# Loading the last rows of w2: 128 overlapping rows in 128 partitions instead of 96 rows in 96 partitions

## The chip, the cores and the metric

One core of one Trainium2 chip runs the whole kernel. The metric is the device time of one execution in microseconds (us). The core has five instruction streams: TensorE (PE in the profile, its weight loads PEld), VectorE (DVE), ScalarE (ACT), GpSimd (POOL) and SyncE (SP). Transfers are carried out by the core's 16 DMA engines; SyncE, ScalarE and GpSimd only put them into queues. Semaphores order everything: an instruction may wait until a semaphore has reached a value, and adds to one when it is done.

## The reference

The kernel computes one decode step of a gated mix of two branches for a single token x of 512 numbers: attention over a cache of 32 heads with 4096 keys and values each (branch a), and a small network with a squared ReLU (branch b). All inputs are bf16. Only branch b is touched here.

```python
g = _sigmoid((x * gate_w).sum(-1, keepdims=True))
a = _A_ref(x, A_k_cache, A_v_cache, A_wq, A_wo)   # q = x @ wq; softmax(q k^T) v per head; @ wo
# branch b: w1 is 512 x 1376, w2 is 1376 x 512
h = jnp.einsum("bsd,df->bsf", x, w1) + b1
r = jnp.where(h > zero, h, zero)
h = r * r
b = jnp.einsum("bsf,fd->bsd", h, w2) + b2
return g * a + (1 - g) * b
```

## The kernel before

The kernel reads the caches of keys and values once, 78.3 MB with all the weights, and works on what has arrived. The 32 heads are taken in 8 tiles of 4 heads. A tile of keys (k) or values (v) is 4 MB: 128 partitions with 32 KB each. Tiles live in a ring of five slots. SyncE issues the loads in a written order (`LOADS`): k0, k1, then k and v alternating, and before the last tile v7 the entry "m", which is branch b's weights. Before an issue it waits until the slot's old tile has been used (`free`).

For each key tile, VectorE computes scores of 80 of the 128 key blocks (L717: a multiply and a sum along the row in one instruction), and TensorE does the other 48: it transposes them (L508), ScalarE copies them out of PSUM (L414), and TensorE multiplies with the queries (L523). ScalarE takes the exponentials (L433), and TensorE multiplies them with the value tiles (L554, `pv`). The work on values stands far behind the work on keys in TensorE's order, which is written out by hand.

The last value tile v7 is loaded in four parts, of 40, 36, 32 and 20 blocks (`PARTS`), each with a semaphore of its own, so that TensorE can begin when the first has landed. In the order of SyncE's queue the end is: w1 (L335, 11,008 bytes for each of 128 partitions), the first 1280 rows of w2 (L336, 10,240 bytes for each partition, ten rows side by side), the 96 rows of w2 that are left (L337, 1,024 bytes for each of 96 partitions), the four parts of v7 (L330; 10,240, 9,216, 8,192 and 5,120 bytes for each partition), and the last 512 rows of wo (L339, two loads of 384 and 128 rows with 1,024 bytes each). The rest of wo came earlier, in pieces that SyncE (L326) and GpSimd (L377) issued.

At the end TensorE works in this order: its part of wo's product with the heads 0 to 27 (L584), h of branch b (L599, `mlp_h`, 11 columns of 4 matmuls), the softmax denominators (L563), branch b's product with w2 (L611, `mlp_out`, 11 groups of 4 matmuls), the first two parts of v7 (L554), the part of wo's product that VectorE had summed (L590), the last two parts of v7 (L554), the last four heads' product with wo (L620, `out_b`), and the transpose of the result (L675). VectorE has in this time a share of wo's product (L778, L782), the bias of h (L757), the squared ReLU (L762) and the factor 1 - g (L766), which makes `hs`, and at the very end the heads' normalisation (L747), the sum (L820) and a copy (L822), and SyncE stores the result (L342).

h is kept with 128 partitions and 11 columns: column n below 10 has the elements n, n + 10, and so on of the first 1280, and column 10 has the 96 that are left, in partitions 0 to 95. `b1c` is b1 in the same layout: TensorE turns the row b1 into columns in PSUM (L467), VectorE clears b1c at the start (L681) and copies it out in two pieces (L701, L702). `omg` is 1 - g, the same number in every partition (L695). Two places wait for both copies of b1c: `started` (L310, SyncE and GpSimd wait there before the pieces of wo) and TensorE, before it reuses that bank of PSUM (L475). The names FG = 10 and FR = 96 are the full groups and the rest.

Of the kernel before, what the change touches and what calls it, by code (L numbers as in the profile page):

```python
# [5 lines left out]
def bass_gated_mix__gqa_block_cached__dense_activation_squared_relu__decode_kernel(  # L6
# [15 lines left out]
    fp32 = mybir.dt.float32  # L22
    bf16 = mybir.dt.bfloat16
    ALU = mybir.AluOpType
# [5 lines left out]
    DM = 512  # L30
    F = 1376
    FG = 10
    FR = F - FG * 128
    SCALE = float(D) ** -0.5


# [59 lines left out]
    def turns():  # L96
        at, out = 0, []
        for _, e, k, _, _ in RUNS:
            d = (e - at) % 16
            out.append((False, d) if d != 1 else (True, e))  # L100
            at = (e + k) % 16
        return out
# [29 lines left out]
    with ctx:  # L132
        def sb(name, shape, dt):
            return ctx.enter_context(nc.sbuf_tensor(name, shape, dt))
# [4 lines left out]
        def sem(name):  # L139
            return ctx.enter_context(nc.semaphore(name))  # L140
# [3 lines left out]
        def held(kind, j=0):  # L144
            return ring[:, AT[kind, j] % SLOTS, :]
# [4 lines left out]
        W2, W3 = 4 * F, 4 * F + FG * DM  # L150
        w1_sb = held("m")[:, 0:W2].rearrange("p (t n) -> p t n", t=4)
        w2a = held("m")[:, W2:W3].rearrange("p (g n) -> p g n", g=FG)
        w2b = held("m")[0:FR, W3:W3 + DM]
        W4 = W3 + DM
        W5 = W4 + NZ * DM
        wob_sb = held("m")[:, W4:W5].rearrange("p (h n) -> p h n", h=NZ)
# [7 lines left out]
        def early(p, n):  # L164
            at[0] += n
            return start[0:p, at[0] - n:at[0]]

        xrow, grow, b1r, b2r = early(1, DM), early(1, DM), early(1, F), early(4, 128)
# [5 lines left out]
        xcol = sb("xcol", [128, 4], bf16)  # L174
        xcolf = sb("xcolf", [128, 4], fp32)
        b1c = sb("b1c", [128, FG + 1], fp32)
# [22 lines left out]
        omg = sb("omg", [128, 1], fp32)  # L199
        hr = sb("hr", [128, FG + 1], fp32)  # L200
        hp = sb("hp", [128, FG + 1], fp32)
        hs = sb("hs", [128, FG + 1], bf16)
        b2g = sb("b2g", [128, 4], fp32)
        fin = sb("fin", [128, 4], bf16)

# [16 lines left out]
        H = pX[:, 256:256 + FG + 1]  # L222
        MO = pX[:, 288:292]
        B1 = pM[:, 288:288 + FG + 1]
# [8 lines left out]
        s_dz = sem("s_dz")  # L233
        s_b = sem("s_b")
        s_l = [sem(f"s_l{i}") for i in range(SLOTS)]
        s_w = [sem(f"s_w{n}") for n in range(3)]
# [8 lines left out]
        s_b1c = sem("s_b1c")  # L245
# [13 lines left out]
        s_g = sem("s_g")  # L259
# [24 lines left out]
        s_hs = sem("s_hs")  # L284
# [14 lines left out]
        def free(eng, n):  # L299
            if n < SLOTS:  # L300
                return
            kind, j = LOADS[n - SLOTS]
            if kind == "k":
                eng.wait_ge(s_sd, U * (j + 1))
                eng.wait_ge(s_t, 2 * U * (j + 1))
            elif kind == "v":
                eng.wait_ge(s_pv, U * (j + 1))


        def started(eng):  # L310
            eng.wait_ge(s_qps, NT)
            eng.wait_ge(s_g, 4)
            eng.wait_ge(s_b1c, 2)


        @block.sync
        def _(eng):
            for n, (kind, j) in enumerate(LOADS):
                free(eng, n)
                if n == SLOTS - 1:  # L320
                    started(eng)
                    for p, st, k, q in STRIPS[len(RUNS):]:
                        a, b = W[p:p + st * (k - 1) + 1:st, :], woa_v[q:q + k, :]
                        if k == 1:
                            a, b = [v.rearrange("p (a n) -> p a n", a=2) for v in (a, b)]
                        eng.dma_start(a, b).then_inc(s_wr, 16)  # L326
                if kind == "v" and j in PARTS:
                    for w in range(len(PARTS[j]) - 1):
                        part = slice(PARTS[j][w] * 128, PARTS[j][w + 1] * 128)
                        eng.dma_start(held("v", j)[:, part], v_v[j][:, part]).then_inc(s_vl[j, w], 16)  # L330
                elif kind in "kv":
                    eng.dma_start(held(kind, j), (k_v if kind == "k" else v_v)[j])\
                       .then_inc(s_l[n % SLOTS], 16)
                elif kind == "m":
                    eng.dma_start(held("m")[:, 0:W2], w1_v).then_inc(s_w[0], 16)  # L335
                    eng.dma_start(held("m")[:, W2:W3], w2_v).then_inc(s_w[1], 16)  # L336
                    eng.dma_start(w2b, B_w2[FG * 128:F, :]).then_inc(s_w[2], 16)  # L337
            for c in range(len(TS) - 1):
                eng.dma_start(wob_sb[:, TS[c]:TS[c + 1], :], wob_v[:, TS[c]:TS[c + 1], :])\  # L339
                   .then_inc(s_wo[c], 16)  # L340
            eng.wait_ge(s_f4, 1)
            eng.dma_start(out[0, 0, :].rearrange("(j p) -> j p", p=128), fin4).then_inc(s_out, 16)  # L342
# [46 lines left out]
        def _(eng):  # L389
# [33 lines left out]
            def exps(j):  # L423
# [7 lines left out]
                for r in range(R):  # L431
                    rows = slice(P * r, P * r + P)
                    eng.activation(E[rows, j % NE, :, r], S[rows, j % NS, :], ACT.Exp,  # L433
                                   bias=nM[rows, j:j + 1], scale=SCALE,
                                   accum_out=RS[rows, R * j + r:R * j + r + 1]).then_inc(s_e, 1)
# [17 lines left out]
        def _(eng):  # L453
# [3 lines left out]
            for t in range(4):  # L457
                mm = eng.matmul(XC[:, t:t + 1], xrow[:, t:DM:4], ident[0:1, 0:1], start=True, stop=True)
# [4 lines left out]
            eng.wait_ge(s_b, 32)  # L463
            eng.transpose(B2, b2r, ident[0:4, 0:4]).then_inc(s_b2, 1)
            for n in range(FG + 1):
                M = 128 if n < FG else FR
                mm = eng.matmul(B1[0:M, n:n + 1], b1r[:, n:FG * 128:FG] if n < FG else b1r[:, FG * 128:F],  # L467
                                ident[0:1, 0:1], start=True, stop=True)
            mm.then_inc(s_b1, 1)
            eng.wait_ge(s_wq, 16)  # L470
# [1 line left out]
            eng.wait_ge(s_ez, 1)  # L472


            read = [(s_b1c, 2)]  # L475

            def pm(sem, count):
                for w in read:
# [114 lines left out]
            def mlp_h():  # L593
                eng.wait_ge(s_w[0], 16)
                for n in range(FG + 1):
                    M = 128 if n < FG else FR
                    for t in range(4):
                        lhs = w1_sb[:, t, n:FG * 128:FG] if n < FG else w1_sb[:, t, FG * 128:F]
                        mm = eng.matmul(H[0:M, n:n + 1], lhs, xcol[:, t:t + 1],  # L599
                                        start=(t == 0), stop=(t == 3))  # L600
                mm.then_inc(s_h, 1)

            def mlp_out():
                eng.wait_ge(s_w[1], 16)
                eng.wait_ge(s_w[2], 16)
                eng.wait_ge(s_hs, 1)
                for n in range(FG + 1):
                    M = 128 if n < FG else FR
                    w = w2a[:, n, :] if n < FG else w2b
                    for j in range(4):  # L610
                        mm = eng.matmul(MO[:, j:j + 1], w[:, j * 128:(j + 1) * 128], hs[0:M, n:n + 1],  # L611
                                        start=(n == 0 and j == 0), stop=(n == FG and j == 3),
                                        skip_group_check=True)
                mm.then_inc(s_mo, 1)
# [47 lines left out]
            spread_a()  # L662
            out_a()
            mlp_h()
            den(NG - 1)
            mlp_out()
            for u in range((NT - 1) * U, NU):
                if u == NU - 2:
# [9 lines left out]
        @block.vector  # L678
        def _(eng):
            eng.memset(zeros, 0.0).then_inc(s_dz, 1)  # L680
            eng.memset(b1c[:, :], 0.0).then_inc(s_dz, 1)  # L681
            eng.wait_ge(s_dz, 2)
            eng.wait_ge(s_x, 32)
            eng.tensor_tensor_reduce(grow, xrow, grow, 1.0, 0.0, ALU.mult,
                                     ALU.add, zp[:, :]).then_inc(s_zp, 1)
# [12 lines left out]
            eng.tensor_scalar(b2g[:, :], B2, omg[:, 0:1], None, ALU.mult).then_inc(s_g, 1)  # L698

            eng.wait_ge(s_b1, 1)  # L700
            eng.tensor_copy(b1c[:, 0:FG], B1[:, 0:FG]).then_inc(s_b1c, 1)  # L701
            eng.tensor_copy(b1c[0:FR, FG:FG + 1], B1[0:FR, FG:FG + 1]).then_inc(s_b1c, 1)  # L702

            def qcol_copy(c):
                eng.wait_ge(s_q, c + 1)
# [20 lines left out]
            def gmax(j):  # L726
                eng.wait_ge(s_mt, j + 1)
                if j >= 2:
# [5 lines left out]
                eng.tensor_scalar(gx[0:1, j % 2, :].rearrange("a (r p) -> a r p", r=R),  # L734
                                  g.unsqueeze(2).to_broadcast([1, R, P]), -SCALE, None, ALU.mult)\
                   .then_inc(s_dg, 1)
# [15 lines left out]

            def mlp_bias():
                eng.wait_ge(s_h, 1)
                eng.wait_ge(s_b1c, 2)
                for p, n in cells:
                    eng.tensor_tensor(hr[p, n], H[p, n], b1c[p, n], ALU.add).then_inc(s_hv, 1)  # L757

            def mlp():
                eng.wait_ge(s_hv, 1)  # L760
                for p, n in cells:
                    eng.scalar_tensor_tensor(out=hp[p, n], in0=hr[p, n], scalar=0.0, in1=hr[p, n],  # L762
                                             op0=ALU.max, op1=ALU.mult).then_inc(s_hv, 1)
                eng.wait_ge(s_hv, 2)
                for p, n in cells:
                    eng.tensor_scalar(hs[p, n], hp[p, n], omg[p, 0:1], None, ALU.mult).then_inc(s_hs, 1)  # L766

            def rows_v():
                eng.wait_ge(s_ac, 3)
# [84 lines left out]
```

## Time and profile before

| What | Value |
|---|---|
| median of three runs | 193.84 us (193.66 to 194.28) |
| the profiled execution, its own time | 194.1 us |
| its span in the profile | 192.7 us |
| VectorE busy | 157.3 us (82%) |
| TensorE busy, weight loads | 111.8 us, 99.3 us |
| ScalarE busy, GpSimd busy | 84.4 us, 22.6 us |
| read from HBM | 78.32 MB, 406 GB/s over the span |
| TensorE's granted clock, mean | 0.584 of full speed |

The span is what the profiler records, from the first instruction to the last; the execution's own time has 1.4 us around it. The profile cuts the span in 40 equal slices of 4.8 us and gives for each the busy share of every engine, the share of the DMA engines and what they moved. The chain of waits is followed back from the last instruction: at each step to what released it, or to the instruction before it. In lines of the chain, "DMA ring<-in_A_v_cache_dram" is the time from a load's issue to its landing, "SPq" is SyncE issuing, and "issue" is time in which an engine waited for nothing that the profile shows. A group such as "L554 x17" is 17 instructions of line 554.

### The profile page before, as it was taken

Reading aid. Unit: us, or ns where it says so; the run is one execution under the profiler, and the core shown is the slowest. Engines: PE = TensorE matmul, PEld = TensorE weight load, DVE = VectorE, ACT = ScalarE, POOL = GpSimd, SP = SyncE. Lnnn points to the kernel's source line nnn. Section 1 sums busy time; section 2 is a strip of 40 time slices with the busy share of each in tenths; the row PEclk is TensorE's granted clock in tenths of the full one; section 3 lists DMA queues with packets and bytes.
Section 4 is the critical chain, followed back from the end, with each engine's and each line's share of the span. In section 5 each row is a group of like instructions: output and inputs, shape, how many; then the busy total and the mean of one; then the engine's idle time right before and its main releaser. Section 6 shows DMA issues by size and latency. Waiting matters only on the chain.

```text
span 192.7 us, 6055 instructions
## 1 busy us (share of the span) xinstructions
PE 111.8 (58%) x2082; PEld 99.3 (52%) x2082; DVE 157.3 (82%) x1357; ACT 84.4 (44%) x204; POOL 22.6 (12%) x56
## 2 busy tenths in 40 slices
PE   0129665545604644396569055925886489769755
PEld 0123343435503543296559045924876378658754
DVE  0220399999999999899999998998999799938821
ACT  2004776734833753087349132933644295031000
POOL 7760001994000000000000000000000000000000
PEclk9999998555555555555555555555555555555555
DMA  6999999999999999999999999999999999999990
GB/s 218 436 435 435 435 437 425 437 468 400 429 427 415 408 451 425 432 410 432 429 424 408 425 434 422 430 434 435 432 420 408 422 410 413 429 415 377 418 367 31
DMA packets 5456, 78.71 MB, mean 408 GB/s; under 512 B 1285, under 2 KB 1895, under 8 KB 2024
## 3 DMA queue, kind: packets, MB, share of 16 engines
q1 hardware_dynamic: 4452, 75.37, 92.6%
q0 software_dynamic: 960, 2.95, 3.9%
q8 instruction: 16, 0.26, 0.6%
q14 instruction: 14, 0.11, 0.1%
q10 hardware_dynamic: 14, 0.01, 0.0%
HBM read 78.32 MB, written 0.00 MB: 406 GB/s over the span
## 4 chain that ended last, share of the span: by engine, by line
DVE 48%; DMA 42%; PE 5%; SPq 2%; issue 2%; DVEq 0%
DVE ring L717 44%; DMA ring<-in_A_k_cache_dram 26%; DMA ring<-in_A_v_cache_dram 16%; PE pO L554 2%; DVE S L717 2%; PE pQ L590 1%; SPq L330 1%; PE KP L508 1%; SPq L336 1%; DVE gm L731 1%; DVE gx L734 0%; PE pQ L620 0%; PE pM L535 0%; PE pM L563 0%; SPq L337 0%
## 5 line engine op out<-in xcount | busy, mean ns | idle before, releaser
L717 DVE CUSTOM_DVE_ANT_0 ring<-ring,qb 128x128 bf16<-128x128 bf16 x640 | 137.2, 280 | 2.6 <-DMA ring<-in_A_k_cache_dram 2.6
L414 ACT ACTIVATE kT<-KP 128x768 bf16<-128x768 bf16 x64 | 48.1, 810 | 49.2 <-PE KP L508 48.8
L508 PE MATMUL KP<-ident,ring 128*128 128x128 bf16 x384 | 45.1, 302 | 23.2 <-DMA ring<-in_A_k_cache_dram 20.5
L508 PEld LDWEIGHTS KP<-ident,ring 128*128 128x128 bf16 x384 | 37.6, 140 | 25.4 <-DMA ring<-in_A_k_cache_dram 20.9
L717 DVE DVE_READ_ACCUMULATOR2_ANT S<- 128x1 f32 x640 | 48.8, 76 | 0.1
L554 PE MATMUL pO<-E,ring 128*128 128x4 bf16 x640 | 19.7, 166 | 4.0 <-DMA ring<-in_A_v_cache_dram 3.0
L554 PEld LDWEIGHTS pO<-E,ring 128*128 128x128 bf16 x640 | 18.9, 105 | 4.5 <-DMA ring<-in_A_v_cache_dram 3.2
L433 ACT ACTIVATE E<-S,nM 32x128 bf16<-32x128 f32 x32 | 18.5, 578 | 0.9
L554 PE MATMUL pX<-E,ring 128*128 128x4 bf16 x384 | 12.0, 167 | 1.6 <-DMA ring<-in_A_v_cache_dram 1.5
L554 PEld LDWEIGHTS pX<-E,ring 128*128 128x128 bf16 x384 | 11.6, 105 | 2.0 <-DMA ring<-in_A_v_cache_dram 1.8
L530 PE MATMUL pM<-identf,mp 128*1 128x128 f32 x8 | 3.1, 384 | 12.8 <-DVE mp L724 12.8
L535 PE MATMUL pM<-onesf,gx 1*128 1x1 f32 x16 | 4.7, 358 | 9.5 <-DVE gx L734 9.5
L535 PEld LDWEIGHTS pM<-onesf,gx 1*128 1x128 f32 x16 | 4.0, 307 | 10.5 <-DVE gx L734 10.5
L523 PE MATMUL pQ<-qcol,kT 128*128 128x4 bf16 x192 | 8.3, 169 | 1.1 <-ACT kT L414 1.1
L523 PEld LDWEIGHTS pQ<-qcol,kT 128*128 128x128 bf16 x192 | 8.0, 110 | 1.4 <-ACT kT L414 1.3
L782 DVE SCALAR_TENSOR_TENSOR ring<-W,o2f,ring 128x512 f32<-128x512 bf16 x11 | 8.3, 751 | 0.4
L425 ACT ACTIVATE nM<-pM 128x1 f32<-128x1 f32 x8 | 1.4, 171 | 15.6 <-PE pM L535 15.6
L433 ACT ACTIVATION_READ_ACCUMULATOR E<-S,nM 32x1 f32 x32 | 8.1, 252 | 0.0
L377 POOL DMA_DIRECT2D W<-in_A_wo_dram x14 | 8.0, 574 | 0.0
L530 PEld LDWEIGHTS pM<-identf,mp 128*1 128x1 f32 x8 | 0.7, 92 | 13.9 <-DVE mp L724 13.9
L523 PE MATMUL pS<-qcol,kT 128*128 128x4 bf16 x192 | 7.9, 168 | 0.0
L385 POOL MEMSET tick<- 1x1 f32 x1 | 0.1, 89 | 66.6 <-DMA W<-in_A_wo_dram 66.6
(83 smaller groups left out, 97.6 us busy)
## 6 DMA issues: line engine op xcount, KB each, us to landing
ring<-in_A_k_cache_dram SPq DMA_DIRECT2D x8, 4096.0 KB, 30.5
ring<-in_A_v_cache_dram SPq DMA_DIRECT2D x5, 4096.0 KB, 29.8
ring<-in_A_v_cache_dram SPq DMA_DIRECT2D x5, 1024.0 KB, 28.5
W<-in_A_wq_dram SPq DMA_DIRECT2D x1, 4096.0 KB, 12.5
ring<-in_A_v_cache_dram SPq DMA_DIRECT2D x2, 2048.0 KB, 27.8
W<-in_A_wo_dram POOLq DMA_DIRECT2D x2, 768.0 KB, 18.1
ring<-in_B_w_dram SPq DMA_DIRECT2D x1, 1376.0 KB, 24.8
ring<-in_B_w_dram SPq DMA_DIRECT2D x1, 1280.0 KB, 27.9
```

Source lines behind the costliest of these rows:

```text
L330: eng.dma_start(held("v", j)[:, part], v_v[j][:, part]).then_inc(s_vl[j, w], 16)
L336: eng.dma_start(held("m")[:, W2:W3], w2_v).then_inc(s_w[1], 16)
L377: eng.dma_start(W[p:p + st * (k - 1) + 1:st, :], woa_v[q:q + k, :], max_dma_last_dim=16384).then_inc(s_wp[n], 16)
L414: eng.activation(kT[:, n % NC, :], KP[n % 3][:, :], ACT.Copy).then_inc(s_ev, 1)
L433: eng.activation(E[rows, j % NE, :, r], S[rows, j % NS, :], ACT.Exp, bias=nM[rows, j:j + 1], scale=SCALE, accum_out=RS[rows, R * j + r:R * ...
L508: mm = eng.transpose(KP[n % 3][:, y * 128:(y + 1) * 128], held("k", j)[:, b * 128:(b + 1) * 128], ident[:, :])
L523: mm = eng.matmul(S2[j % 2][:, c:c + R], kT[:, n % NC, y * 128:(y + 1) * 128], qcol[:, R * j:R * j + R], start=True, stop=True)
L530: eng.transpose(MT[0:1, :], mp[:, j:j + 1], identf[:, :]).then_inc(s_mt, 1)
L535: eng.matmul(MB[:, j:j + 1], gx[0:1, j % 2, :], onesf[0:1, 0:1], start=True, stop=True).then_inc(s_mb, 1)
L554: mm = eng.matmul(O(R * j, R * j + R), held("v", j)[:, b * 128:(b + 1) * 128], E[:, j % NE, b, :], start=(b == 0), stop=(b == B - 1), skip ...
L717: ins = eng.tensor_tensor_reduce(kb, kb, qb[:, j, :], 1.0, 0.0, ALU.mult, ALU.add, S[:, j % NS, b:b + 1])
L782: eng.scalar_tensor_tensor(out=vsum[:, :], in0=wo_sb[:, TP + t, :], scalar=o2f[:, t:t + 1], in1=vsum[:, :], op0=ALU.mult, op1=ALU.add).the ...
```

## The change

The last load of w2 takes the last 128 rows, 1248 to 1375, into 128 partitions. The first 32 of them, rows 1248 to 1279, are also among the 1280 rows loaded by L336. Column 10 of h is computed for the same 128 elements, so that every matmul of branch b has 128 columns or 128 rows. A new tile `omw` is 1 - g in all 128 x 11 places but the first 32 partitions of column 10, where it is zero; `hs` is the product with omw in place of the product with omg, so the overlapping rows count once. b1c is filled completely by one copy, and need not be cleared; the two waits on it ask for one copy. VectorE gets one instruction more in all; the instructions of the other engines stay as many.

```diff
--- before.py
+++ after.py
@@ -31,6 +31,8 @@
     F = 1376
     FG = 10
     FR = F - FG * 128
+
+    FO = 128 - FR
     SCALE = float(D) ** -0.5
 
 
@@ -150,7 +152,7 @@
         W2, W3 = 4 * F, 4 * F + FG * DM
         w1_sb = held("m")[:, 0:W2].rearrange("p (t n) -> p t n", t=4)
         w2a = held("m")[:, W2:W3].rearrange("p (g n) -> p g n", g=FG)
-        w2b = held("m")[0:FR, W3:W3 + DM]
+        w2b = held("m")[:, W3:W3 + DM]
         W4 = W3 + DM
         W5 = W4 + NZ * DM
         wob_sb = held("m")[:, W4:W5].rearrange("p (h n) -> p h n", h=NZ)
@@ -200,6 +202,7 @@
         hr = sb("hr", [128, FG + 1], fp32)
         hp = sb("hp", [128, FG + 1], fp32)
         hs = sb("hs", [128, FG + 1], bf16)
+        omw = sb("omw", [128, FG + 1], fp32)
         b2g = sb("b2g", [128, 4], fp32)
         fin = sb("fin", [128, 4], bf16)
 
@@ -310,7 +313,7 @@
         def started(eng):
             eng.wait_ge(s_qps, NT)
             eng.wait_ge(s_g, 4)
-            eng.wait_ge(s_b1c, 2)
+            eng.wait_ge(s_b1c, 1)
 
 
         @block.sync
@@ -334,7 +337,7 @@
                 elif kind == "m":
                     eng.dma_start(held("m")[:, 0:W2], w1_v).then_inc(s_w[0], 16)
                     eng.dma_start(held("m")[:, W2:W3], w2_v).then_inc(s_w[1], 16)
-                    eng.dma_start(w2b, B_w2[FG * 128:F, :]).then_inc(s_w[2], 16)
+                    eng.dma_start(w2b, B_w2[F - 128:F, :]).then_inc(s_w[2], 16)
             for c in range(len(TS) - 1):
                 eng.dma_start(wob_sb[:, TS[c]:TS[c + 1], :], wob_v[:, TS[c]:TS[c + 1], :])\
                    .then_inc(s_wo[c], 16)
@@ -463,8 +466,7 @@
             eng.wait_ge(s_b, 32)
             eng.transpose(B2, b2r, ident[0:4, 0:4]).then_inc(s_b2, 1)
             for n in range(FG + 1):
-                M = 128 if n < FG else FR
-                mm = eng.matmul(B1[0:M, n:n + 1], b1r[:, n:FG * 128:FG] if n < FG else b1r[:, FG * 128:F],
+                mm = eng.matmul(B1[:, n:n + 1], b1r[:, n:FG * 128:FG] if n < FG else b1r[:, F - 128:F],
                                 ident[0:1, 0:1], start=True, stop=True)
             mm.then_inc(s_b1, 1)
             eng.wait_ge(s_wq, 16)
@@ -472,7 +474,7 @@
             eng.wait_ge(s_ez, 1)
 
 
-            read = [(s_b1c, 2)]
+            read = [(s_b1c, 1)]
 
             def pm(sem, count):
                 for w in read:
@@ -593,10 +595,9 @@
             def mlp_h():
                 eng.wait_ge(s_w[0], 16)
                 for n in range(FG + 1):
-                    M = 128 if n < FG else FR
                     for t in range(4):
-                        lhs = w1_sb[:, t, n:FG * 128:FG] if n < FG else w1_sb[:, t, FG * 128:F]
-                        mm = eng.matmul(H[0:M, n:n + 1], lhs, xcol[:, t:t + 1],
+                        lhs = w1_sb[:, t, n:FG * 128:FG] if n < FG else w1_sb[:, t, F - 128:F]
+                        mm = eng.matmul(H[:, n:n + 1], lhs, xcol[:, t:t + 1],
                                         start=(t == 0), stop=(t == 3))
                 mm.then_inc(s_h, 1)
 
@@ -605,10 +606,9 @@
                 eng.wait_ge(s_w[2], 16)
                 eng.wait_ge(s_hs, 1)
                 for n in range(FG + 1):
-                    M = 128 if n < FG else FR
                     w = w2a[:, n, :] if n < FG else w2b
                     for j in range(4):
-                        mm = eng.matmul(MO[:, j:j + 1], w[:, j * 128:(j + 1) * 128], hs[0:M, n:n + 1],
+                        mm = eng.matmul(MO[:, j:j + 1], w[:, j * 128:(j + 1) * 128], hs[:, n:n + 1],
                                         start=(n == 0 and j == 0), stop=(n == FG and j == 3),
                                         skip_group_check=True)
                 mm.then_inc(s_mo, 1)
@@ -678,8 +678,9 @@
         @block.vector
         def _(eng):
             eng.memset(zeros, 0.0).then_inc(s_dz, 1)
-            eng.memset(b1c[:, :], 0.0).then_inc(s_dz, 1)
+            eng.memset(omw[:, :], 1.0).then_inc(s_dz, 1)
             eng.wait_ge(s_dz, 2)
+            eng.memset(omw[0:FO, FG:FG + 1], 0.0).then_inc(s_dz, 1)
             eng.wait_ge(s_x, 32)
             eng.tensor_tensor_reduce(grow, xrow, grow, 1.0, 0.0, ALU.mult,
                                      ALU.add, zp[:, :]).then_inc(s_zp, 1)
@@ -698,8 +699,9 @@
             eng.tensor_scalar(b2g[:, :], B2, omg[:, 0:1], None, ALU.mult).then_inc(s_g, 1)
 
             eng.wait_ge(s_b1, 1)
-            eng.tensor_copy(b1c[:, 0:FG], B1[:, 0:FG]).then_inc(s_b1c, 1)
-            eng.tensor_copy(b1c[0:FR, FG:FG + 1], B1[0:FR, FG:FG + 1]).then_inc(s_b1c, 1)
+            eng.tensor_copy(b1c[:, :], B1).then_inc(s_b1c, 1)
+            eng.wait_ge(s_dz, 3)
+            eng.tensor_scalar(omw[:, :], omw[:, :], omg[:, 0:1], None, ALU.mult).then_inc(s_g, 1)
 
             def qcol_copy(c):
                 eng.wait_ge(s_q, c + 1)
@@ -752,7 +754,7 @@
 
             def mlp_bias():
                 eng.wait_ge(s_h, 1)
-                eng.wait_ge(s_b1c, 2)
+                eng.wait_ge(s_b1c, 1)
                 for p, n in cells:
                     eng.tensor_tensor(hr[p, n], H[p, n], b1c[p, n], ALU.add).then_inc(s_hv, 1)
 
@@ -762,8 +764,9 @@
                     eng.scalar_tensor_tensor(out=hp[p, n], in0=hr[p, n], scalar=0.0, in1=hr[p, n],
                                              op0=ALU.max, op1=ALU.mult).then_inc(s_hv, 1)
                 eng.wait_ge(s_hv, 2)
+                eng.wait_ge(s_g, 5)
                 for p, n in cells:
-                    eng.tensor_scalar(hs[p, n], hp[p, n], omg[p, 0:1], None, ALU.mult).then_inc(s_hs, 1)
+                    eng.tensor_tensor(hs[p, n], hp[p, n], omw[p, n], ALU.mult).then_inc(s_hs, 1)
 
             def rows_v():
                 eng.wait_ge(s_ac, 3)
```

## The prediction

> **What bounds the kernel now.** I read the page first: its span, its DMA rows and the shares of the chain that ended last.
>
> ```profile
> span 192.7 us, 6055 instructions
> DMA  6999999999999999999999999999999999999990
> GB/s 218 436 435 435 435 437 425 437 468 400 429 427 415 408 451 425 432 410 432 429 424 408 425 434 422 430 434 435 432 420 408 422 410 413 429 415 377 418 367 31
> q1 hardware_dynamic: 4452, 75.37, 92.6%
> DVE 48%; DMA 42%; PE 5%; SPq 2%; issue 2%; DVEq 0%
> ```
>
> The 16 DMA engines are 9 tenths or more busy in 38 of 40 slices, and queue q1, which SyncE fills, has 92.6% of their time. VectorE's 48% of the chain is the pacing of ring slots; the engines do not run dry for it. A slice is 4.8 us. Slice 37 (173.4 to 178.2 us) moves 377 GB/s between 415 and 418, with the engines still fully busy.
>
> Next, the chain in order of time from 149 us, which shows what the last load releases (columns: start, length, what):
>
> ```profile
> 149.98 0.33 SPq L335
> ...
> 150.35 1.09 SPq L336
> ...
> 151.49 0.43 SPq L337
> ...
> 153.59 30.89 DMA ring<-in_A_v_cache_dram
> ...
> 184.52 0.61 PE pO L554 x17
> 185.14 0.81 issue
> 185.95 0.67 PE pO L554 x19
> 186.62 1.71 PE pQ L590 x8
> 188.32 1.40 PE pO L554 x52
> ...
> 190.09 0.60 PE pQ L620 x16
> ```
>
> L337 is the load in question. It stands in q1 ahead of all four parts of the last V tile, and the end hangs on the second part, which lands at 184.5 us. After that TensorE works to the end, with one pause of 0.81 us put down to no wait. So what lengthens or shortens the engines' work between L337 and the second V part moves the end by as much.
>
> Then the table of windows, which places the slow stretch (length, busy time and count of five engines, TensorE's clock, DMA share, GB/s):
>
> ```profile
> 171.00:174.40 3.40, 2.39 (x50) 2.00 (x51) 0.94 (x5) 2.48 (x9) 0.00 (x0) 0.50 1.00 422
> 174.40:178.10 3.70, 3.70 (x108) 3.70 (x104) 3.52 (x6) 0.00 (x0) 0.00 (x0) 0.50 1.02 366
> 178.10:181.20 3.10, 2.70 (x62) 2.58 (x60) 2.46 (x6) 0.00 (x0) 0.00 (x0) 0.50 1.00 418
> ```
>
> The packet records of the trace, one for each row piece that an engine moves, say what lies there. L337's 96 packets of 1,024 B start between 174.45 and 178.00 us: the engines reach this load one after another, up to 3.5 us apart. The loads beside it (the body of w2 and the first V part) have 256 packets of 10,240 B, 388 ns each when undisturbed; 84 of them took over 5% longer, up to 654 ns, and all 84 start between 174.68 and 178.04 us. Of the next 9,216 B and 5,120 B packets, none of 256 did. So the fall to 366 GB/s has the place of L337, and goes when it goes.
>
> **The change, part by part.** *The load.* 96 rows over 16 engines are 6 packets for each (the slowest engine has exactly 6 there), 128 rows are 8. In a run of them one 1,024 B packet follows the other by about 43 ns, so the added work is 2 x 43 = 86 ns on every engine: +0.09 us on the path.
>
> *The slow stretch.* The 84 slowed packets took 6.70 us more than 388 ns each, and L337's own slowed packets (46 ns undisturbed, up to 134 ns) 0.66 us more: 7.36 us over 16 engines is 0.46 us for each. The windows say the same: 3.70 us at 366 GB/s instead of 420 (the mean of the neighbours) lose 3.70 x 54/420 = 0.48 us. The engine that ends last, which sets the landing, went from the end of w1 (174.30 us) to the end of the first V part (181.17 us) in 6.87 us; undisturbed this would be 2 x 3.06 us (eight 10,240 B packets) and 6 x 43 ns, 6.38 us, so it lost 0.49 us. Does a load of 128 rows cost this too? The trace has one of the very form that L337 gets: the last load of L339, 128 rows of 1,024 B, with the 384 rows of its first part ahead of it. Their 512 packets run from 185.09 to 189.37 us, and of the 88 V packets of 5,120 B that start in that stretch none took over 206 ns (196 ns at least). I therefore take the whole 0.46 us as gone. The bounds are 0.49 us gone, and nothing gone but 8/6 of it: 0.61 us, 0.15 us more than now.
>
> [...]
>
> *TensorE.* The number of matmuls stays; one at L467, four at L599 and four at L611 get 128 columns or rows for 96. L599 takes 2.82/44 = 64 ns each; a third of that on four is 0.09 us, of L611 (1.31/44 = 30 ns) 0.04. After L611 TensorE waits 0.45 us for the first V part, and that wait shrinks to 0.08 us when the part comes 0.37 us earlier. If L611 ended 0.1 us later, the 40 products of the first part would, too: they take 1.23 us from 181.67, against 1.62 us of idle time before the second part. Nothing on the path.
>
> *VectorE at the start.* The new memset and the memset of the 32 zero weights (0.07 us, the row of the replaced memset) lie in its 7.26 us of waiting for x. One copy of b1 in place of two (0.17 and 0.14 us) and the product omw x omg (0.15 to 0.24 us, by L695 and L766) end by 14.6 us; its next instruction, the copy of qcol, waits until 17.62 us. Uncovered, they are +0.1 us. b1c comes no later than now: TensorE (L493) asks for it at 17.08 us, and SyncE and GpSimd ask beside the q projections, which run past 30 us.
>
> *VectorE at the end.* The product into hs becomes a tensor_tensor of 128x11 (0.17 us at L757, against 0.24 us at L766 now). Its added wait on s_g = 5 was met at 14.6 us. Behind it stand the six products of L782, which end at 184.35 us, while L590 uses them from 186.48 us: 2.1 us of cover.
>
> *SyncE.* The issue of L337 takes 0.43 us. [...]
>
> **Sum.** 194.1 us (the profiled execution: span 192.7 and 1.4 around it) + 0.09 - 0.46 = 193.73 us. wo's last packet ends at 189.37 us and moves along, as do L554, L590 and L620. The median of the runs shown, 193.84, is 0.26 below the profiled execution: 193.5 us.
>
> **The rivals.** *Nothing of the slow stretch belongs to 96 rows* (another traffic of that moment makes it, say the 16,384 B instruction packet at 174.98 us; it stays): +0.09 us, 193.9. For it: that packet and two long TensorE groups lie there. Against it: the same kind of packet at 183.46 us slowed a single V packet. [...] *Slower: the loss belongs to short rows among long ones, whatever their number.* Place: the same stretch; price: 0.15 + 0.09 = +0.24 us, 194.1; it decides once the slowed packets cost more than 0.46 - 0.09 = 0.37 us per engine. For it: the engines are 3.5 us apart at either load. Against it: wo's 512 packets. *The pause holds.* If the 0.81 us pause ends at its own time (an instruction packet ended at 184.5 us, shortly before it) and not 0.81 us after the landing, all behind it stays: 0, 193.8. *A second such pause* behind the landing: -0.37 + 0.81 = +0.44, 194.3; one was seen in 192.7 us, and the count of TensorE's instructions stays. *More than the mean:* the pause goes, and the slowest engine also comes level with the second (its second V part ends at 183.61 against 183.96 us, 0.35 us). TensorE would then wait for wo, which lands some 0.1 us ahead of its use now: -0.37 - 0.1 - up to 0.25, 193.1.
>
> **How the numbers follow.** Forecast 193.5: 0.46. No loss by form: 0.14. Short rows: 0.12. Pause holds: 0.08. Second pause: 0.07. More than the mean: 0.13. Medians of the kernel before lie within 0.3 us, and each case has that spread. A 0.3% (0.58 us) is about what a measurement of this kernel can tell from no change: below 193.26 or above 194.42. Faster gets a quarter of the forecast and most of the last case, 0.22; slower a part of the second pause and of the short rows, and what I do not see, 0.11; the rest, 0.67, is within. The range takes in 193.1 less a part of its spread, and the second pause: 192.9 to 194.4. The forecast's own range is 193.2 to 193.8.
>
> **What would show it.** Right: the window of the load moves about 420 GB/s; slice 37 loses its dip; hardly any 10,240 B packet is over 407 ns; the second V part releases L554 at about 184.15 us, and wo's last packet ends at 189.0. Wrong: the dip stays or deepens with 128 packets in it; or it goes and L554's second group still starts near 185.95 us.

## The result and the profile after

| | before | changed |
|---|---|---|
| median | 194.08 us (193.66 to 194.57) | 193.45 us (193.20 to 193.92) |
| profiled execution, its span | 194.1, 192.7 us | 193.29, 191.9 us |

The ratio is 0.9975, with a 95% interval of 0.9964 to 0.9985: 0.49 us faster (0.29 to 0.70). In a second comparison it was 0.9987 (0.9975 to 0.9999).

The DMA row of the changed kernel's page, GB/s in 40 slices, has lost its dip: slice 37 moved 377 and moves 416.

```profile
GB/s 219 438 437 437 437 439 427 439 418 439 413 439 424 420 439 406 427 415 437 403 453 427 427 408 437 435 425 437 427 418 417 413 420 406 425 416 416 416 384 50
```

The table of windows shows the same (length, busy time and count of five engines, TensorE's clock, DMA share, GB/s). The stretch of the load went from 366 to 412 GB/s:

```profile
171.00:174.40 3.40, 2.43 (x66) 1.98 (x67) 1.37 (x6) 2.48 (x9) 0.00 (x0) 0.50 1.00 419
174.40:178.10 3.70, 3.70 (x98) 3.70 (x96) 3.56 (x5) 0.00 (x0) 0.00 (x0) 0.50 1.02 412
178.10:181.20 3.10, 2.27 (x62) 2.13 (x62) 2.66 (x7) 0.00 (x0) 0.00 (x0) 0.50 1.01 422
```

Of the 256 packets of 10,240 B, 10 are slowed by more than 5%, where 84 were. The load's own packets lose 0.002 us in all, where they lost 0.68; but in a second profile of the changed kernel they lose 0.58, so that part does not belong to the load's form.

The chain in order of time (start, length, what; L556 is L554 of before):

```profile
153.34 30.38 DMA ring<-in_A_v_cache_dram
...
183.77 0.62 PE pO L556 x17
184.39 0.79 issue
185.18 0.67 PE pO L556 x19
```

The second V part is used 0.75 us earlier than before (184.52), the pause is still there, and the span is 0.78 us shorter. This looks like the forecast. But two things in it do not fit. TensorE had been 0.52 us ahead already at 168.6 us, before the changed load. And L611 starts 0.77 us earlier (179.14 for 179.91), though it waits for no V part. The timelines of before and of the changed kernel, at the landing of an earlier V tile (in brackets the idle time before, and what ended it):

```profile
169.16 0.99 PE L554 MATMUL pX<-E,ring 128*128 128x4 bf16 x31 [1.54 <-DMA ring<-in_A_v_cache_dram]
```

```profile
168.64 1.01 PE L556 MATMUL pX<-E,ring 128*128 128x4 bf16 x32 [1.50 <-DMA ring<-in_A_v_cache_dram]
```

That raised the question of what the end really hangs on.

### The profile page after: what moved, and what is told of

It is laid out like the page before. It is cut to its first block, busy times and chain, and to the rows that moved or that the text cites. A ratio compares the mean times of both kernels' runs of the same rounds, so it can differ in the third digit from the quotient of the medians.

```text
span 191.9 us, 6054 instructions
## 1 busy us (share of the span) xinstructions
PE 112.0 (58%) x2080; PEld 99.3 (52%) x2082; DVE 157.2 (82%) x1358; ACT 84.5 (44%) x204; POOL 22.8 (12%) x56
## 4 chain that ended last, share of the span: by engine, by line
DVE 48%; DMA 42%; PE 5%; SPq 2%; issue 1%; DVEq 0%
DVE ring L719 45%; DMA ring<-in_A_k_cache_dram 26%; DMA ring<-in_A_v_cache_dram 16%; PE pO L556 2%; DVE S L719 2%; SPq L333 1%; PE pQ L592 1%; PE KP L510 1%; DVE gm L733 1%; DVE gx L736 0%; PE pQ L620 0%; PE pM L537 0%; PE pM L565 0%; SPq L339 0%; SPq L340 0%
## 5 line engine op out<-in xcount | busy, mean ns | idle before, releaser
L719 DVE DVE_READ_ACCUMULATOR2_ANT S<- 128x1 f32 x640 | 51.0, 80 | 0.1
L556 PE MATMUL pO<-E,ring 128*128 128x4 bf16 x640 | 19.7, 166 | 4.4 <-DMA ring<-in_A_v_cache_dram 3.1
L556 PEld LDWEIGHTS pO<-E,ring 128*128 128x128 bf16 x640 | 18.9, 105 | 4.9 <-DMA ring<-in_A_v_cache_dram 3.3
L556 PE MATMUL pX<-E,ring 128*128 128x4 bf16 x384 | 12.0, 167 | 1.8 <-DMA ring<-in_A_v_cache_dram 1.8
L556 PEld LDWEIGHTS pX<-E,ring 128*128 128x128 bf16 x384 | 11.6, 105 | 2.2 <-DMA ring<-in_A_v_cache_dram 2.0
```

What stands on the lines that cost most here:

```text
L556: mm = eng.matmul(O(R * j, R * j + R), held("v", j)[:, b * 128:(b + 1) * 128], E[:, j % NE, b, :], start=(b == 0), stop=(b == B - 1), skip ...
L719: ins = eng.tensor_tensor_reduce(kb, kb, qb[:, j, :], 1.0, 0.0, ALU.mult, ALU.add, S[:, j % NS, b:b + 1])
```

## The experiments

### Which part of the change makes the gain?

Theory: the load's form. Rival: the other edits. First the changed kernel with only its load undone:

```diff
-                    eng.dma_start(w2b, B_w2[F - 128:F, :]).then_inc(s_w[2], 16)
+                    eng.dma_start(w2b[FO:128, :], B_w2[FG * 128:F, :]).then_inc(s_w[2], 16)
```

> The changed kernel in all but the load: the last 96 rows of w2 go into partitions 32 to 127, and partitions 0 to 31 keep finite numbers of an old key tile, which omw weights by zero. Theory (a load of 96 rows makes the DMA engines slow each other, 0.46 us for each): the slow stretch is back, with over 50 of the 10,240 B packets slowed by more than 5% and some 7 us of lost time over 16 engines, and the time is that of the kernel before, ratio 0.999 to 1.001. Rival (the gain comes from the other edits: one copy for b1c, tensor_tensor with omw, matmuls of 128): no slowed packets matter, ratio 0.997 to 0.998 as the changed kernel. Second rival (only partitions 0 to 95 are bad): no slowed packets, ratio 0.9965 to 0.997, since each engine has two packets less than in the changed kernel.

Measured: 193.79 us, ratio 0.9991 (0.9981 to 1.0002); 121 packets slowed. The slow stretch is back as expected, at other partitions too. The time is within what the theory gave, but its interval still overlaps that of the changed kernel, so it does not clearly go back.

Then the kernel before with only the load changed:

```diff
-                    eng.dma_start(w2b, B_w2[FG * 128:F, :]).then_inc(s_w[2], 16)
+                    eng.dma_start(held("m")[:, W3:W3 + DM], B_w2[F - 128:F, :]).then_inc(s_w[2], 16)
```

> The kernel before in all but the load: rows 1248 to 1375 of w2 go into 128 partitions, and the product still takes the first 96 partitions, so that the last group of branch b is multiplied with rows 1248 to 1343 of w2 in place of 1280 to 1375. Theory: the load alone makes the gain, ratio 0.997 to 0.998, at most 10 packets of 10,240 B slowed, the window of the load at 410 to 420 GB/s. Rival (the other edits make it): ratio 0.999 to 1.001.

Measured: 193.81 us, ratio 0.9995 (0.9984 to 1.0006); 9 packets slowed, and 405 GB/s in the window, a little under what was expected. The load does to the DMA engines what was forecast, and the time hardly moves, as the rival had it. The theory falls here.

### What does such a load cost the DMA engines?

Four more loads behind the first, of 96 or of 128 rows:

```diff
+                    for c in range(4):
+                        spare = held("m")[0:96, 13568 + c * DM:13568 + (c + 1) * DM]
+                        eng.dma_start(spare, B_w2[F - 96:F, :]).then_inc(s_dup, 16)
```

> The kernel before with four more loads of the same 96 rows, right behind the first, into columns of the slot that nothing reads. Theory: each costs 6 packets of 43 ns, 0.26 us, and 0.46 us by slowing, 0.72 us: +2.9 us in all, ratio 1.015, and five times the slowed packets' excess, some 35 us over 16 engines. Rival (the slowing belongs to that moment, not to the load): 4 x 0.26 = +1.0 us, ratio 1.005, the excess as before, some 7 us.

> The kernel before with four more loads of 128 rows of the same bytes per row, right behind the 96 rows, into columns of the slot that nothing reads. Theory: each costs 8 packets of 43 ns, 0.34 us, and slows nothing: +1.4 us, ratio 1.007, less than with four more loads of 96 rows although it moves a third more. Rival (short rows among long ones are slow whatever their number): 0.34 and 0.61 us each, +3.8 us, ratio 1.020, more than with 96 rows.

Measured: with 96 rows 196.12 us, ratio 1.0113 (1.0098 to 1.0128); with 128 rows 194.77 us, ratio 1.0045 (1.0030 to 1.0060). The window of the loads (174.4 to 178.1 us) with four more of 96 rows, then with four more of 128:

```profile
174.40:178.10 3.70, 3.70 (x99) 3.70 (x97) 3.56 (x5) 0.00 (x0) 0.00 (x0) 0.50 1.05 266
```

```profile
174.40:178.10 3.70, 3.70 (x100) 3.70 (x97) 3.56 (x5) 0.00 (x0) 0.00 (x0) 0.50 1.03 340
```

The same DMA engines, as busy, move 266 or 340 GB/s. By the packet records, the stretch from the last packet of w1 to the last of the second V part, which holds the rest of w2, the loads in question and two V parts, is 9.61 to 9.84 us in the five profiles with one load of 96 rows and 9.32 to 9.34 in the six with one of 128. With four more it is 12.35 (96 rows: 0.67 us each) and 11.09 us (128 rows: 0.36 each, where 8 packets of 43 ns make 0.34). What slowed packets lose, over all engines, is 36 us with four more of 96 rows and 9 us with four more of 128, for 7.4 before. So the forecast's prices for the engines hold, and the rival by which short rows are slow in any number is out. But the kernels' times grew less than the engines' work: by 2.2 us (0.0113 x 194) for 2.7, by 0.9 for 1.4. So some 0.5 us were hidden by something.

### What hides it: the pause

In the traces so far the pause of TensorE between the groups of 17 and 19 products is 0.79, 0.81, 0.39 or 1.33 us long, and gone with four more loads. The packet records have one 16,384 B packet of the instruction queue shortly before it. From those records and the timelines (us):

| kernel | L611 starts | instruction packet | second V part used | pause ends | pause | span |
|---|---|---|---|---|---|---|
| before | 179.91 | 183.46 to 184.52 | 184.52 | 185.95 | 0.81 | 192.7 |
| changed | 179.14 | 182.67 to 183.74 | 183.77 | 185.18 | 0.79 | 191.9 |
| changed, load of 96 | 179.89 | 183.26 to 184.33 | 184.65 | 185.65 | 0.39 | 192.4 |
| before, load of 128 | 180.18 | 183.68 to 184.74 | 184.28 | 186.22 | 1.33 | 193.0 |

The pause ends 1.3 to 1.5 us after the packet, whenever the V part lands, and the span ends 6.7 us after the pause. The packet starts 3.4 to 3.6 us after L611. So Theory A: TensorE waits for its own instructions, of which each packet brings a block, and the end hangs on what comes before L611. Theory B is the forecast's: the landing of the second V part sets the end.

A second place in the traces fits Theory A. In the third and fourth kernel of the table TensorE also stops for about a quarter of a microsecond after 20 of the 44 products of L599 (the third row's L600 takes 2.81 us, the second row's 2.58). From there to the pause it is 127 products with their weight loads, 254 instructions. This stop, and an earlier V tile that landed at 169.14 us for 168.64, are why L611 starts so much later in the third row than in the second.

If the pause is bound to a place in TensorE's order of instructions, more instructions at the start must move it. Twenty matmuls, 40 instructions with their weight loads, while TensorE waits for x:

```diff
             eng.wait_ge(s_id, 3)
+            for n in range(20):
+                eng.matmul(pX[:, 320:321], ident[:, :], ident[:, 0:1], start=True, stop=True)
             eng.wait_ge(s_x, 32)
```

> The changed kernel itself, beside the three next ones on one chip, with a new profile. Ratio 0.9975 within 0.001, as before. Theory A (the pause of 0.8 us in TensorE's stream ends 1.4 us after the end of its 16,384 B instruction packet, and the end of the kernel is that moment and 6.7 us): in the new profile, too, the pause ends 1.3 to 1.5 us after the end of the packet that starts near 183 us, whatever its length, and the span ends 6.7 us later. Theory B (the landing of the second V part sets the end, the pause follows it with a fixed length): the pause is 0.8 us long again.

> The changed kernel with 20 more matmuls into an unused column of PSUM at the start, where TensorE waits for x. They move every later instruction by 40 places against the 16,384 B pieces in which TensorE's program comes. Theory A: the piece that ended in the middle of the second V part now ends in the last blocks of the first, its packet is asked for before L611 and not after it, and the wait for it lies under the wait for the second V part; no pause between the group of 17 and that of 19, the end then hangs on the landings of the second V part and of wo, 0.2 to 0.3 us earlier than the changed kernel: ratio 0.996 to 0.9967. Theory B: the pause stays behind the landing, ratio 0.9975.

> The kernel before with the same 20 matmuls. Theory A: no pause; the end hangs on the landing of wo, which was used within 0.2 us of its landing: 0.1 to 0.3 us faster than before, ratio 0.9985 to 0.9995. The changed kernel with the shift against this one is then the forecast's own sum, the DMA engines' 0.46 - 0.09 = 0.37 us: 0.998. Theory B: ratio 1.000.

> The kernel before with the load of 128 rows alone (the product takes rows 1248 to 1343 of w2 for its last group in place of 1280 to 1375) and the same 20 matmuls. Theory A: with no pause to hide it, the load alone gives what the whole change gives: as the changed kernel with the shift, ratio 0.996 to 0.997. Rival (the other edits make part of the gain even without the pause): between this and the kernel before with the shift, 0.998 or above.

Measured: changed again 193.68 us, 0.9987 (0.9975 to 0.9999), pause 0.85 us, 1.48 us after its packet; changed and shifted 193.23 us, 0.9963 (0.9950 to 0.9976); before, shifted 193.61 us, 0.9989 (0.9971 to 1.0006); load alone, shifted 193.18 us, 0.9965 (0.9952 to 0.9979). In the timeline of the changed and shifted kernel, the products of the V parts (L558 there) are cut at another place:

```profile
182.42 1.13 PE L558 MATMUL pO<-E,ring 128*128 128x4 bf16 x37
184.11 1.20 PE L558 MATMUL pO<-E,ring 128*128 128x4 bf16 x39 [0.56 <-issue]
```

The cut came after 40 + 17 products and comes after 37: 20 products, 40 instructions earlier, exactly. The packet starts at 181.56 us, 1.1 us earlier than in the changed kernel. That is Theory A's mark. Its expectation was wrong in one thing: the pause did not vanish, and the end does not hang on the landings, so that the ratios came out as expected by another course. The place 127 products ahead of the cut is now the start of L602 (L599 of before), and the chain of the changed and shifted kernel, which has a pause of 0.75 us there, shows that course:

```profile
177.18 0.75 issue
177.93 2.56 PE pX L602 x44
...
184.94 0.76 DVE ring L787
185.75 1.87 PE pQ L594 x8
```

Branch b starts at 177.93 us, 2.1 us later than in the changed kernel: TensorE stood 0.75 us here, and 0.83 us among the products of an earlier V tile, from 169.8 us. VectorE waits for h with its last six products (L787), and TensorE waits for VectorE's sum (L594). So these three kernels have another bound than the others, and the forecast's sum cannot be read from them as I had meant. Load alone against before, both shifted, is 0.0024 lower, with an error as large (0.0022); in their profiles both have the second V part early enough, and the difference in span (192.0 and 192.2) is that of the moment when TensorE goes on after the pause before L601 (177.68 and 177.89 us). What the load has to do with that stays open.

### Length before L611, work before the landing

The last four kernels test both theories with larger prices. The kernel before with five groups of L599 96 columns wide, and with two more loads of 128 rows:

```diff
-                    M = 128 if n < FG else FR
+                    M = 128 if n < FG - 4 else FR
...
-                        lhs = w1_sb[:, t, n:FG * 128:FG] if n < FG else w1_sb[:, t, FG * 128:F]
+                        lhs = w1_sb[:, t, n:n + FG * (M - 1) + 1:FG] if n < FG else w1_sb[:, t, FG * 128:F]
```

> The kernel before with five of the eleven groups of L599 96 columns wide in place of one; 128 of the 1,376 elements of h are left out (those of the last 32 partitions in columns 6 to 9). In the two profiles a group of four matmuls with 96 columns takes 0.2 us longer than one with 128, so L599 should take up to 0.8 us more. Theory A (the end hangs on TensorE's instruction packet, which comes 3.5 us after the start of L611, and so on all that L611 waits for): the end moves by as much as L599 gets longer, up to +0.8 us, ratio 1.002 to 1.0045. Theory B (the end hangs on the landing of the second V part): 0.8 us lie inside the idle time before the V parts, ratio 1.000.

Measured: 195.83 us, ratio 1.0102 (1.0086 to 1.0119). L599 takes 4.52 us for 2.82, 1.70 us more: twice the price I had taken from the one group, whose columns lie side by side, where those of the four new groups lie ten apart. The end moves by 1.98 us (1.67 to 2.31). The chain:

```profile
184.14 0.61 PE pO L554 x17
184.75 2.57 issue
187.33 0.67 PE pO L554 x19
```

The V part is used earlier than in the profile of before (184.14 for 184.52), and the kernel is 2 us slower: the pause took it. L611 starts at 181.29, the packet at 184.78, the pause ends 1.49 us after the packet. Theory B, by which those 1.7 us lie in idle time and the ratio is 1.000, is out.

> The kernel before with two more loads of 128 rows behind the first, into columns that nothing reads: the DMA engines have 2 x 0.35 us more to do before the V parts. Theory A: the second V part lands 0.7 us later, the pause of 0.8 us gets shorter by that, and the end stays: ratio 0.9995 to 1.001, and the pause is 0.0 to 0.3 us in the profile. Theory B: +0.7 us, ratio 1.0036, and the pause is 0.8 us.

Measured: 194.12 us, ratio 1.0012 (1.0001 to 1.0024), where B has 1.0036. The engines' stretch is 10.31 us, 0.65 more than before's. The chain has the pause at 0.48 us, longer than the 0.3 that I expected, and its end at 185.75:

```profile
184.65 0.61 PE pO L559 x17
185.27 0.48 issue
185.75 0.67 PE pO L559 x19
```

In this execution w1 ended 0.47 us earlier than in that of before (173.83 for 174.30), so that the second V part is used only 0.13 us later; this is why the pause is longer than expected. Of 0.65 us of DMA work 0.23 us (0.02 to 0.47) are seen: most is hidden, and I can't say that all is.

> The changed kernel with the load of 96 rows into partitions 32 to 127, once more, for a narrower interval. Theory A: the 128-column group in L599 (0.21 us) and the product into hs (0.07 us) shorten what comes before L611 by 0.28 us, the load has no part in it: ratio 0.9986 within 0.0008. Theory B (the load makes the gain): 1.000.

Measured: 193.62 us, ratio 0.9987 (0.9976 to 0.9999), as Theory A has it.

> The kernel before with the load of 128 rows alone (the product takes rows 1248 to 1343 of w2 for its last group), once more, for a narrower interval. Theory A: the second V part lands 0.3 us earlier, the pause gets longer by that, ratio 1.000 within 0.0008. Theory B: 0.9975 to 0.998.

Measured: 193.84 us, ratio 1.0001 (0.9991 to 1.0011): the load alone gives nothing, and B's 0.9975 is outside. In its profile the second V part is used at 184.04 and the pause is 0.87 us.

## Why the prediction was right or wrong

The time was forecast at 193.5 us and came at 193.45, but the gain was made by other parts of the change than those that I gave it to. That the number came so near is luck: 0.31 us which I had priced at nothing stand where I had put the load's 0.37 us. The base moved too, from 193.84 us in the forecast to 194.08 in the comparison.

**The load's price was right.** +0.09 and -0.46 us for each DMA engine, -0.37 in sum; the profiles have 9.33 us for 9.67 in the stretch, -0.34. (The 0.49 us that the slowest engine was said to lose took eight packets of 388 ns for 3.06 us; they make 3.10, and the loss 0.40.) Its cause in the number of rows is shown, by one load undone, one alone, and four more of either kind. No run shows why 96 rows slow 84 of the 256 packets beside them, and 128 rows 10.

**The step that failed is the first one:** "the end hangs on the second part, which lands at 184.5 us". After that landing stood a pause of 0.81 us, and I let it move with the landing. It ends 1.2 to 1.5 us after an instruction packet, whenever the V part lands, and so 0.8 us of room lay behind the landing. The rival "the pause holds" had this, at 0.08, and gave 193.8: what the load alone measured (193.81 and 193.84). What spoke for it was in view: the prediction itself had dated an instruction packet to 184.5 us, shortly before the pause ended. The end of a stage that pauses for nothing that the profile shows need not be set by what released it.

**TensorE's edit was mis-priced in sign and in place.** I gave the 128 columns in L599 a third more time, 0.09 us, and called it hidden. They took less. The groups of weight loads by form, of the kernel before and of the changed one (busy us, mean ns of one, idle us before):

```profile
L599 PEld LDWEIGHTS pX<-xcol,ring 128*128 128x128 bf16 x40 | 2.4, 156 | 0.0
L599 PEld LDWEIGHTS pX<-xcol,ring 128*96 128x96 bf16 x4 | 0.4, 193 | 0.0
```

```profile
L600 PEld LDWEIGHTS pX<-xcol,ring 128*128 128x128 bf16 x44 | 2.5, 152 | 0.0
```

The four loads of 96 columns, which lie side by side, take 193 ns each; those of 128 columns ten apart take 156. The second mean still mixes two kinds: by the records of the single loads, the 128 columns of the changed kernel's last group, which lie side by side, take 124, 103, 104 and 104 ns. Such loads overlap, and by the same records one product follows the other by 80 ns in the group of 96 columns, by 58 in those of 128 columns ten apart, and by 26 in the new last group: 4 x 54 ns are 0.22 us, and the line went from 2.82 to 2.58 us. I had read the mean over all. Side by side, then, 96 columns take nearly twice as long as 128 (193 ns for 104). They take longer where the columns lie ten apart, too, in the kernel with five groups of 96:

```profile
L599 PEld LDWEIGHTS pX<-xcol,ring 128*96 128x96 bf16 x20 | 3.1, 247 | 0.0
L599 PEld LDWEIGHTS pX<-xcol,ring 128*128 128x128 bf16 x24 | 1.5, 155 | 0.0
```

Of these 20 loads of 96 columns, four have them side by side (176 to 197 ns); the 16 with columns ten apart take 258 to 262 ns, and one product follows the other by 167 ns there, where 128 columns ten apart have 58: 16 x 109 ns are 1.74 us, for the 1.70 that L599 took longer.

**VectorE's product into hs** was priced right, 0.17 for 0.24 us, and put off the path; L611 waits for it. The timelines of before and of the changed kernel:

```profile
179.53 0.24 DVE L766 TENSOR_SCALAR hs<-hp,omg 128x11 bf16<-128x11 f32 x1
```

```profile
178.82 0.17 DVE L769 TENSOR_TENSOR hs<-hp,omw 128x11 bf16<-128x11 f32 x1
```

I had asked only which data wait for L611, and found 0.45 us of cover. But the instruction packet starts 3.4 to 3.6 us after L611 in nine profiles, and the last pause ends 1.2 to 1.5 us after the packet, so what L611 waits for counts as well.

**The sum as the runs have it** is 0.24 + 0.07 = 0.31 us before L611, and the load nothing: 0.9984. The other edits without the load measured 0.9991 and 0.9987, which agrees; the whole change 0.9975 and 0.9987, and 0.9984 is just inside the first one's interval (to 0.9985). That the two profiles differ by more, 0.78 us, comes from an earlier place: 0.52 us of it are there at the landing of the V tile at 168.64 us for 169.16, and the changed kernel's second profile has this landing at 169.01. From it to the end of the span it is 23.53 us before and 23.26 and 23.27 us in the changed kernel's two profiles, 0.27 less.

The two parts of the sum are less sure than the whole. No run has either of them alone. The nine profiles do not tell whether the packet follows the start of L611 or the end of L599, since both keep their distance to it within 0.25 us, so the 0.07 us are argued and not shown. And the two profiles of the other edits alone show no gain up to L611: from that landing it is 10.75 us, as before, because L600 has the stop after 20 products there. What the wider group saves shows only between profiles that are alike in this: L600 takes 2.58 us for L599's 2.82 without a clear stop, 2.81 and 2.86 for 3.05 and 3.10 with it.

The edits at the start, on SyncE's queue and the added wait have no term in the forecast's sum, and no run has them alone.

**A faster version.** The changed kernel with 20 matmuls at the start measured 193.23 us against 193.68 for the changed kernel in the same comparison (0.9963, 0.9950 to 0.9976, against 0.9987, 0.9975 to 0.9999). Work that computes nothing helps here; it moved the places where TensorE pauses, the last from after 57 products of the V parts to after 37 (0.85 us long there, 0.56 here). The kernel before with the load alone gains from it as well (0.9965).

## What to carry to other kernels

A pause that no semaphore explains, in the middle of a group of equal instructions, is a bound to be dated before anything ahead of it is costed: look for an instruction packet shortly before its end (1.2 to 1.5 us here), and ask what that packet came after (L611's start here, by 3.4 to 3.6 us). A landing that comes earlier between the packet and such a pause was worth nothing here (1.0001 with the load alone), while work ahead of the packet counted (1.70 us longer in L599, 1.98 us later at the end). Weight loads and transfers of an odd shape are priced by their own form, never by the mean of a line: 193 ns for a weight load of 96 columns here, where the mean of L599's 44 loads is 159.

## What the runs showed of the hardware

- The profile's instruction queue q8 moves packets of 16,384 B (16 of them in the kernel before), which take 1.0 to 1.3 us each in the last 20 us of these kernels. That the packet shortly before the pause is TensorE's own is inferred from the times: in nine profiles the last pause ended 1.2 to 1.5 us after it, and it started 3.4 to 3.6 us after L611. 40 more instructions moved the place of the pause by 40.
- Each of four more loads of 96 rows of 1,024 B (partitions 0 to 95) among larger ones made the DMA engines' stretch 0.67 us longer, each of four more of 128 rows 0.36, though it moves a third more. With the one load's 96 rows in partitions 32 to 127 the stretch is as long (9.61 and 9.84 us, for 9.32 to 9.34 with 128 rows).
- A weight load of 96 columns took 193 ns with the columns side by side and about 260 with them ten apart, one of 128 columns 104 and 157, at a granted clock of 0.50. Products with such loads followed each other by 80 and 167 ns, with 128 columns by 26 and 58.
